# Contiguous block transposes of the probabilities, V's rows loaded to match them, and a new order of steps in a fused attention and expert kernel

## The chip, the cores and the metric

The kernel runs on 1 core of one Trainium2 chip. The metric is the device time of one launch in microseconds; the kernel before takes 739.89 us, the median of 3 runs (739.19 to 741.18). Each engine of the core runs its own instructions in order and waits on semaphores for the others: TensorE (PE in the profile, with its weight loads as PEld), VectorE (DVE), ScalarE (ACT), GpSimd (POOL), and SyncE (SP), which here issues nearly all DMA transfers.

## The reference, cut to what is computed

```python
B, H, S, D = 8, 8, 576, 64                     # pool = 8, so 72 keys for each head
k_p = k.reshape(B, H, 72, 8, D).mean(axis=3)
v_p = v.reshape(B, H, 72, 8, D).mean(axis=3)
scores = (q @ k_p.transpose(0, 1, 3, 2)) / sqrt(D)
attn = exp(scores - max(scores)); attn = attn / (sum(attn) + 1e-9)
x = (attn @ v_p).transpose(0, 2, 1, 3).reshape(4608, 512)
a = x @ w1; b = x @ w2                          # 512 -> 1024 each
out = ((a * b) @ w3) @ w_out                    # 1024 -> 1024 -> 512
```

All inputs and the output are fp32.

## The kernel before

**Numbers.** Every operand of a product is split into a rounded high part and the rest, and three products (high by high, high by low, low by high) stand for one in fp32. So nearly every result of PE is followed by a cast on ACT (the high part, `*_hi`, `*_post`) and a subtraction on DVE or POOL (the low part, `*_lo`).

**Stages.** The 4608 tokens are 12 chunks of 384. From the start to about 83 us W = w3 @ w_out is made (`w_turn`, `w_mm`; the conversions are `high`, `low`, `conv_b`, `ro_hi`, `ro_lo`, where `low` runs on DVE at L199 or on ACT at L196). Chunks 0 to 3 then run plain: `ab` (a and b, twelve matmuls of 128 x 384 each per block of 128 hidden columns), `a_post`, `b_post` (L807, a times b), `g_hi` (L812), `g_lo` (L817), `out_t` (L835). Chunks 4 to 11 run in pairs from about 320 us: seven block products stand for eight (`prod`, L976), on sums of the weights' blocks that were mixed before (`mix_sum`, `mix`, `plain_out`) and written to DRAM, one tensor `ws` for each block j of hidden columns. `load_u` (L958) brings them back into a ring of 5 buffers of 512 KB (and one of 256 KB); a load waits until the products have left its buffer. The last stage writes the rest of the output.

**Attention of a chunk** runs ahead of its expert stage, between the other steps: scores (`s_mm`), softmax (`soft1`, `soft_e`, `soft_s`, `soft2`; on the tiles in `SOFT_ACT` part of it runs on ACT), then the probabilities are turned so that keys lie on partitions. A pair of heads has 144 keys: the middle 128 are `main`, and the 16 outer ones of all four pairs are gathered into R (`soft3`, `soft4`). For chunks 0 and 1 PE turns them. For the others `te_turn` does it on DVE, as 32 x 32 blocks: one instruction for `main` at L674, which reads the keys interleaved (`(e k)`, k = 4), and two for R at L677. `te_in` (L696) then spreads the blocks over the partitions by DMA, `te_post` splits them, and `av_mm` (L739) multiplies by V's pooled means: `vbd`, block-diagonal for a pair of heads, with a high part (`prep_v2`, L494, ACT) and a low part (`prep_v3`, L499, DVE or POOL), and `VR` for the outer keys (`prep_vr2`). `load_v` (L471) loads half of a batch's V by one 512 KB transfer; `pool_tree` sums groups of 8 rows.

**What sets the order.** Each step is put into `plan` by `at(kind, k, fn, args)`, and a table, `SEQUENCE`, a permutation of the plan's indices, gives the order in which all steps are written; each engine, SP's transfers included, runs its instructions in that order. A second table, `OTHER`, moves single steps to another engine (`on()`: from DVE to POOL; `low` and `out_post`: from DVE to ACT). Output rows leave through a ring of 3 buffers: `out_post` (L866 on ACT, L868 on DVE) copies and at once issues the store (L869).

Of the kernel before, what the change touches and what calls it, by code (L numbers as in the profile page):

```python
# [19 lines left out]
def kernel(  # L20
# [48 lines left out]
        "mix": {(0, 0), (1, 1), (3, 0), (4, 0), (4, 1), (5, 0), (5, 1), (7, 0), (7, 1)},  # L69
        "mix_sum": {(0, 0), (1, 0), (1, 1), (2, 0), (3, 0), (3, 1), (4, 0), (4, 1), (5, 0), (5, 1), (6, 1), (7,  # L70
            0)},
        "out_post": {(0, 0), (0, 1), (0, 2), (1, 1), (1, 2), (2, 1), (2, 2), (3, 1), (3, 2), (4, 0), (4, 2), (5,
            0), (5, 1), (6, 0), (6, 2), (7, 0), (7, 2), (8, 0), (8, 2), (9, 1), (10, 0), (10, 1)},
        "prep_k": {(0, 1), (1, 0), (1, 1), (2, 0), (2, 2), (3, 0), (3, 1), (3, 2), (4, 1), (4, 3), (5, 0), (5,
            1), (5, 2), (5, 3), (6, 0), (6, 2), (6, 3), (7, 0)},
        "prep_v": {(0, 0), (0, 1), (1, 0), (2, 0), (2, 1), (3, 0), (5, 0), (5, 1), (6, 1), (7, 1)},
        "prep_v3": {(0, 0), (1, 0), (1, 1), (2, 1), (3, 0), (4, 0), (4, 1), (7, 0), (7, 1)},
        "prep_vr": {(0,), (1,), (2,), (3,), (5,), (6,), (7,)},
        "prep_vr2": {(0,), (1,), (2,), (3,), (7,)},
        "r3_low": {(0,), (1,), (2,), (4,), (13,), (15,)},  # L80
        "ro_lo": {(4,), (5,), (7,)},
        "ro_low": {(0,), (1,), (2,), (3,), (5,), (7,)},
        "soft4": {(0, 0), (0, 1), (1, 2), (2, 0), (2, 2), (3, 1), (5, 1), (5, 2), (6, 0), (6, 1), (7, 0), (7,
            2), (7, 3), (8, 0), (8, 1), (8, 2), (9, 2), (10, 0), (10, 1), (10, 3), (11, 2)},
        "t_lo": {(0, 0), (0, 1), (1, 0), (1, 1), (2, 1), (3, 0), (3, 1), (4, 0), (5, 1)},
        "t_low": {(0, 0), (0, 1), (1, 1), (3, 1), (5, 1)},
        "vr_sub": {(1,)},
# [29 lines left out]
    msk = small.tile([P, 16], F32, name="msk")[:, :4]  # L117
# [351 lines left out]
    def load_v(b, hf):  # L469
        t = stage["v", b, hf] = st_tile([P, 2, POOL, D])  # L470
        nc.sync.dma_start(out=t.rearrange("k a e d -> k a (e d)"), in_=pair_rows(v, b)[KR:KR + P, 2 * hf:2 * hf + 2])  # L471
# [126 lines left out]
    def soft2(n, t):  # L598
        b, off, nt = tok_tiles(n)[t]
        E, sm = Et[n, t], Mt.pop((n, t))[1]  # L600
        nc.vector.tensor_scalar(
            out=sm[:nt], in0=sm[:nt], scalar1=1e-9, scalar2=float(POOL), op0=ALU.add, op1=ALU.mult)
# [60 lines left out]
    def te_turn(n, t):  # L663
# [6 lines left out]
        if x == 0:  # L670
# [185 lines left out]
    def out_post(m, t):  # L856
# [12 lines left out]
        nc.sync.dma_start(out=out[r0:r0 + P], in_=ob)  # L869
# [354 lines left out]
    for m in range(NP):  # L1224
# [29 lines left out]
    for M in range(NP // 2, NCH // 2):  # L1254
# [78 lines left out]
    for b in range(1, B):  # L1333
# [189 lines left out]
```

## Time and profile before

| what | value |
|---|---|
| median of 3 runs | 739.89 us |
| the profiled execution | 740.11 us |
| its span | 738.3 us |
| TensorE busy | 720.7 us (98%) |
| VectorE busy | 523.8 us (71%) |
| ScalarE busy | 362.1 us (49%) |
| GpSimd busy | 189.1 us (26%) |
| DMA queue 1, share of 16 engines | 63.0% |

A time is the whole execution; the span, from the first to the last recorded instruction, is 1.8 us shorter. The profile names groups of instructions by line, engine, operation and tiles (out<-in), and gives for an idle stretch of an engine the instruction of another engine or the transfer that ended it. PEclk is the granted TensorE clock as a share of full speed.

### The profile page before, as it was taken

The page shows a single profiled execution, that of the slowest core. Times are in us where ns is not written, and L with a number is a line of the kernel's source. Part 1 is how long each engine was busy: PE and PEld are TensorE (multiplying, and loading weights), DVE is VectorE, ACT ScalarE, POOL GpSimd, SP SyncE. Part 2 cuts the span into 40 slices and gives each one's busy share as a digit, 9 for nine tenths or more (in the row PEclk, how much of TensorE's full clock was granted, in tenths as well). Part 3 has the DMA queues.
Part 4 walks back from the last instruction along what each step waited for, and adds up shares of the span by engine and source line. Part 5 has one row for each costly group of instructions (what it writes and reads, how often), then busy time and mean ns, then how long its engine had stood idle before and what let it go on. Part 6 is the DMA issues. An engine that isn't in the chain of part 4 may idle for free.

```text
span 738.3 us, 12016 instructions
## 1 busy us (share of the span) xinstructions
PE 720.7 (98%) x3992; PEld 665.9 (90%) x3992; DVE 523.8 (71%) x1042; ACT 362.1 (49%) x1140; POOL 189.1 (26%) x241
## 2 busy tenths in 40 slices
PE   7999999999999999998999999999999999999997
PEld 6788989899989999998999899899898999899996
DVE  3988898869767968887568877488887576643342
ACT  6888786534334544663355553355554254421221
POOL 2343865434506506203313011220030100000000
PEclk9999999999999999999999999999999999999999
DMA  9999590174457556798785739966358563166511
GB/s 320 348 285 288 154 255 30 59 205 118 108 141 249 155 152 194 198 293 224 221 263 151 186 106 277 252 204 175 86 194 276 139 208 115 34 228 233 173 35 69
DMA packets 138733, 136.59 MB, mean 185 GB/s; under 512 B 76080, under 2 KB 104240, under 8 KB 138672
## 3 DMA queue, kind: packets, MB, share of 16 engines
q1 hardware_dynamic: 138528, 135.69, 63.0%
q8 instruction: 32, 0.52, 0.3%
q14 instruction: 29, 0.24, 0.1%
q10 hardware_dynamic: 144, 0.13, 0.1%
HBM read 99.35 MB, written 24.12 MB: 167 GB/s over the span
## 4 chain that ended last, share of the span: by engine, by line
PE 78%; DVE 9%; DMA 4%; POOL 4%; ACT 3%; issue 2%; SPq 0%; DVEq 0%; POOLq 0%; ACTq 0%
PE a L976 17%; PE o L835 14%; PE att L976 8%; PE o L851 8%; PE a L787 6%; PE b L787 6%; PE b L976 5%; PE att L543 4%; PE att L739 4%; PE o L1068 3%; DMA ring<-ws 2%; DMA PTx<-T 1%; DVE mx L559 1%; POOL VR L530 1%; DMA raw<-in_moe_w_out_dram 1%
## 5 line engine op out<-in xcount | busy, mean ns | idle before, releaser
L976 PE MATMUL a<-X,ring 128*128 128x384 f32 x768 | 157.0, 340 | 1.4 <-DVE g L1009 0.7
L976 PEld LDWEIGHTS a<-X,ring 128*128 128x128 f32 x768 | 134.7, 189 | 7.0 <-DVE g L1009 1.7
L835 PE MATMUL o<-Wc,gh 128*128 128x512 f32 (+1 forms) x384 | 118.6, 390 | 0.0
L581 ACT ACTIVATE E<-att,mx 128x72 f32<-128x72 f32 (+1 forms) x264 | 80.7, 324 | 32.8 <-DVE mx L559 21.2
L482 POOL TENSOR_TENSOR st<-st 72x512 f32<-72x512 f32 (+2 forms) x32 | 42.7, 1335 | 162.0 <-DMA st<-in_v_dram 101.3
L835 PEld LDWEIGHTS o<-Wc,gh 128*128 128x128 f32 x384 | 70.2, 188 | 11.7 <-DVE ob L868 0.2
L976 PE MATMUL att<-X,ring 128*128 128x384 f32 x384 | 78.6, 341 | 2.0 <-DMA ring<-ws 2.0
L835 PE MATMUL o<-Wc,gl 128*128 128x512 f32 (+1 forms) x192 | 74.6, 389 | 1.2 <-DVE gl L817 1.1
L787 PE MATMUL b<-xT,hl 128*128 128x384 f32 x384 | 73.2, 340 | 0.1
L787 PE MATMUL a<-xT,hl 128*128 128x384 f32 x384 | 72.4, 337 | 0.0
L976 PEld LDWEIGHTS att<-X,ring 128*128 128x128 f32 x384 | 68.0, 190 | 3.5 <-DVE R L630 2.4
L787 PEld LDWEIGHTS a<-xT,hl 128*128 128x128 f32 x384 | 66.7, 188 | 0.5
L787 PEld LDWEIGHTS b<-xT,hl 128*128 128x128 f32 x384 | 66.2, 188 | 0.7 <-DVE a L807 0.4
L851 PE MATMUL o<-Wc,gh 128*128 128x512 f32 x192 | 61.6, 393 | 0.0
L817 DVE TENSOR_TENSOR gl<-a,gh 128x384 fp32r<-128x384 f32 x64 | 41.1, 646 | 22.7 <-ACT gh L812 18.2
L581 ACT ACTIVATION_READ_ACCUMULATOR E<-att,mx 128x1 f32 (+1 forms) x264 | 55.2, 209 | 0.0
L812 ACT CAST gh<-a 128x384 fp32r<-128x384 f32 x64 | 33.0, 517 | 43.8 <-DVE a L1004 14.9
L543 PE MATMUL att<-kbd,qT 128*128 128x144 f32 (+1 forms) x320 | 49.3, 286 | 0.6 <-DVE qT L390 0.6
L543 PEld LDWEIGHTS att<-kbd,qT 128*128 128x128 f32 (+1 forms) x320 | 45.3, 179 | 2.9 <-DVE qT L390 0.9
L835 PEld LDWEIGHTS o<-Wc,gl 128*128 128x128 f32 x192 | 36.0, 188 | 10.2 <-DVE gl L817 2.6
L559 DVE TENSOR_REDUCE mx<-att 128x4 f32<-128x288 f32 (+1 forms) x80 | 34.9, 448 | 14.4 <-PE att L543 14.3
L982 ACT COPY a<-a 128x384 f32<-128x384 f32 x32 | 15.3, 479 | 51.5 <-PE a L976 51.3
(164 smaller groups left out, 1348.7 us busy)
## 6 DMA issues: line engine op xcount, KB each, us to landing
ring<-ws SPq DMA_DIRECT2D x81, 512.0 KB
raw<-in_moe_w_dram SPq DMA_DIRECT2D x32, 512.0 KB
ws<-hl SPq DMA_DIRECT2D x24, 512.0 KB
out_dram<-ob SPq DMA_DIRECT2D x35, 256.0 KB
st<-in_v_dram SPq DMA_DIRECT2D x16, 512.0 KB
PTx<-T SPq DMA_DIRECT2D x28, 288.0 KB
ring<-ws SPq DMA_DIRECT2D x29, 256.0 KB
st<-in_k_dram SPq DMA_DIRECT2D x24, 288.0 KB
```

What stands on the lines that cost most here:

```text
L482: eng.tensor_tensor(out=t[:, :, 0:4], in0=t[:, :, 0:4], in1=t[:, :, 4:8], op=ALU.add)
L543: nc.tensor.matmul(out=ps[:nt, 2 * KP * j:2 * KP * (j + 1)], lhsT=qT[n][:, pr, off:off + nt], rhs=kbd[b % 2][:, pr], start=True, stop=True,)
L559: nc.vector.tensor_reduce(out=mx[:nt, hs], in_=sv, axis=AX.X, op=ALU.min)
L581: nc.scalar.activation(out=E[:nt, h], in_=sv[:, i], func=AF.Exp, scale=-1.0, bias=mx[:nt, h:h + 1], accum_out=sm[:nt, h:h + 1])
L739: nc.tensor.matmul(out=Tp[n, pr, "x"][:, off:off + cnt], lhsT=parts[x][0], rhs=parts[x][1], start=x == 0, stop=x == 3)
L787: nc.tensor.matmul(out=o, lhsT=w12[j, w][:, kt, sw], rhs=x[sx][:, kt], start=(i == 0), stop=(i == 3 * NK - 1))
L812: nc.scalar.copy(out=gh, in_=g)
L817: eng.tensor_tensor(out=gl, in0=g, in1=f(gh), op=ALU.subtract)
L835: nc.tensor.matmul(out=o, lhsT=(gh, gl)[sg][:, c], rhs=W[j][sw][:, d], start=(j == 0 and i == 0), stop=(j == NJ - 1 and i == 2))
L851: nc.tensor.matmul(out=oacc[m][t], lhsT=(gh, gl)[sg][:, t * P:(t + 1) * P], rhs=W[j][sw], start=(j == first and i == 0), stop=(j == last a ...
L976: nc.tensor.matmul(out=o, lhsT=w[:, kt, sw], rhs=x[sx][:, kt], start=first and n == 0, stop=n == 5, skip_group_check=True)
L1068: nc.tensor.matmul(out=wacc[h][it], lhsT=w3t[s][sa][:, it * P:(it + 1) * P], rhs=wo[j][sb], start=(j == 0 and i == 0), stop=(j == NJ - 1 a ...
```

## The change

- `te_turn`: for batches b >= 2 `main` is read as it lies, so a block of 32 neighbouring keys is turned as a block (30 of the 33 tiles). The two instructions for R become one of twice the size, on all 33 tiles.
- `load_v`: for b >= 2 V's rows are loaded in the order that this gives the keys, as two transfers of 256 KB in place of one of 512 KB (12 more transfers).
- `prep_v2`, `prep_v3`: with that order the two heads of a pair are no longer in the two halves of the partitions, so for b >= 2 both run over all 128 partitions and multiply by a mask per row (`halves()`, made once by a DVE reduction). `prep_v3` is then on DVE always.
- `soft2`: for n >= 2 and tiles in `SOFT_ACT` (27 tiles) the scaling of the sums moves from DVE to ACT.
- `out_post`: the store of an output tile becomes a step of its own, `out_st`, with its own place in the order (33 stores; those of the last chunk follow their copy as before).
- `OTHER` is dealt anew, and `SEQUENCE` is a new permutation.

Over the kernel PE keeps 3834 instructions; DVE goes from 1044 to 991, ACT from 879 to 910, POOL from 246 to 236, SP from 569 to 581.

```diff
-        "prep_v3": {(0, 0), (1, 0), (1, 1), (2, 1), (3, 0), (4, 0), (4, 1), (7, 0), (7, 1)},
+        "prep_v3": {(0, 0), (0, 1)},
...
-        "ro_low": {(0,), (1,), (2,), (3,), (5,), (7,)},
+        "ro_low": {(1,), (6,)},
...
     def load_v(b, hf):
         t = stage["v", b, hf] = st_tile([P, 2, POOL, D])
-        nc.sync.dma_start(out=t.rearrange("k a e d -> k a (e d)"), in_=pair_rows(v, b)[KR:KR + P, 2 * hf:2 * hf + 2])
+        src = pair_rows(v, b)[KR:KR + P, 2 * hf:2 * hf + 2]
+        if b < 2:
+            nc.sync.dma_start(out=t.rearrange("k a e d -> k a (e d)"), in_=src)
+            return
+        for a in range(2):
+            nc.sync.dma_start(
+                out=t[:, a].rearrange("k e d -> k (e d)"), in_=src[:, a].rearrange("(k p) c -> p k c", k=4))
...
+    def halves():
+        if "halves" not in stage:
+            m = stage["halves"] = masks[:, 4:6]
+            nc.vector.tensor_reduce(
+                out=m, in_=ident.rearrange("p (c j e) -> p j c e", j=2, e=2), axis=AX.XY, op=ALU.add)
+        return stage["halves"]
+
     def prep_v2(b, par):
+        if b >= 2:
+            nc.scalar.mul(
+                out=vbd[b % 2][0][:, :, D * par:D * par + D], in_=vm[b], mul=halves()[:, par:par + 1])
+            return
...
     def prep_v3(b, par):
+        if b >= 2:
+            hi, lo = (vbd[b % 2][s][:, :, D * par:D * par + D] for s in range(2))
+            nc.vector.scalar_tensor_tensor(
+                out=lo, in0=vm[b], scalar=halves()[:, par:par + 1], in1=f(hi), op0=ALU.mult, op1=ALU.subtract)
+            return
...
-        nc.vector.tensor_scalar(
-            out=sm[:nt], in0=sm[:nt], scalar1=1e-9, scalar2=float(POOL), op0=ALU.add, op1=ALU.mult)
+        if n < NT or (n, t) not in SOFT_ACT:
+            nc.vector.tensor_scalar(
+                out=sm[:nt], in0=sm[:nt], scalar1=1e-9, scalar2=float(POOL), op0=ALU.add, op1=ALU.mult)
+        else:
+            nc.scalar.activation(
+                out=sm[:nt], in_=sm[:nt], func=AF.Copy, scale=float(POOL), bias=1e-9 * POOL)
...
         nc.vector.transpose(
-            out=T[:, :, :NPR].rearrange("p k a e -> p a k e"), in_=main.rearrange("p a (e k) -> p a k e", k=4))
-        for s in range(2):
-            nc.vector.transpose(
-                out=T[:, 2 * s:2 * s + 2, NPR:],
-                in_=R[:nt, s].rearrange("p (r e) -> p r e", r=2).unsqueeze(1).broadcast_to([nt, 2, 2, 32]))
+            out=T[:, :, :NPR].rearrange("p k a e -> p a k e"),
+            in_=main.rearrange("p a (e k) -> p a k e", k=4) if b < 2 else main)
+        nc.vector.transpose(
+            out=T[:, :, NPR:],
+            in_=R[:nt].rearrange("p s (r e) -> p s r e", r=2).unsqueeze(2).broadcast_to([nt, 2, 2, 2, 32]))
...
-        nc.sync.dma_start(out=out[r0:r0 + P], in_=ob)
+        stage["ob", m, t] = ob
+        if m == NCH - 1:
+            out_st(m, t)
+
+    def out_st(m, t):
+        r0 = m * CH + t * P
+        nc.sync.dma_start(out=out[r0:r0 + P], in_=stage.pop(("ob", m, t)))
...
     SEQUENCE = (
...
```

**Where the order changes: SP at the start of the pair stage.** A ring load of block j names `ws_93` (j = 0), `ws_94` (j = 1), `ws_95` (j = 2); `st` are K's and V's rows. `ring_3967` of before and `ring_3937` of after are read by the first att product of j = 1, `ring_3942` of before by a product of j = 2. Before:

```order
L958 DMA ring_3871<-ws_93 128x1024
L901 DMA ws_99<-hl_3864 128x4x256
L958 DMA ring_3919<-ws_93 128x1024
L407 DMA st_3921<-in_k_dram 72x2x512
L958 DMA ring_3942<-ws_95 128x1024
L407 DMA st_3953<-in_k_dram 72x2x512
L958 DMA ring_3965<-ws_93 128x512
L958 DMA ring_3967<-ws_94 128x1024
```

and after:

```order
L991 DMA ring_3871<-ws_93 128x1024
L408 DMA st_3911<-in_k_dram 72x2x512
L991 DMA ring_3913<-ws_93 128x1024
L991 DMA ring_3937<-ws_94 128x1024
L902 DMA out_0_dram<-ob_3908 128x512
L991 DMA ring_3966<-ws_93 128x512
L484 DMA st_3972<-in_v_dram 16x1x512 x4
L991 DMA ring_3985<-ws_94 128x1024
```

The first ring load of `ws_94` has moved from the fifth ring load of the group to the third, ahead of the 256 KB load; the load of `ws_95` has left the group, and an output store and four small loads of V's outer rows have come into it.

**ACT before the first product with batch 2's V** (chunk 3; `vm` is the pooled V, `gh` the high part of a times b, `xT0` the high part of that product's result). Before:

```order
L797 COPY a_2465<-a_2450 128x384
L893 CAST hl_2467<-mix_2156 128x4x128
L706 CAST PTh_2406<-PTx_2407 128x768
L812 CAST gh_2520<-a_2465 128x384
L494 CAST vbd0_0_103<-vm_1937 64x4x64
L765 CAST xT0_2533<-att_2528 128x384
```

and after:

```order
L839 CAST gh_2217<-a_2160 128x384
L507 ACTIVATE vbd0_0_103<-vm_1996,msk_109 128x4x64 x2
L824 COPY a_2243<-a_2230 128x384
L599 ACTIVATE E_2189<-E_2189 128x288
L926 CAST hl_2266<-mix_1974 128x4x128
```

The second high part of `vbd` stood right before the cast of the product's first result; now both stand together, and that cast (`xT0_2543`) follows 25 rows later.

**DVE at that same place.** After, the low parts of `vbd` are on DVE, the second right before the subtraction that makes the low part of the product's result:

```order
L734 TENSOR_TENSOR PTx_2392<-PTx_2392,PTh_2391 128x2x384
L895 COPY ob_2497<-o1_2051 128x512
L834 TENSOR_TENSOR a_2492<-b_2499,a_2492 128x384
L517 SCALAR_TENSOR_TENSOR vbd0_1_104<-vm_1996,msk_109,vbd0_0_103 128x4x64
L799 TENSOR_TENSOR xT1_2544<-att_2538,xT0_2543 128x384
```

Before, one of the two was on POOL, behind POOL's `mix` and `VR` work.

**DVE early in the start stage** (`wt` and `Wc` hold raw and converted weights). Before:

```order
L203 SCALAR_TENSOR_TENSOR Wc<-Wc 128x512
L199 TENSOR_SCALAR Wc<-raw 128x512
L203 SCALAR_TENSOR_TENSOR wt<-wt 128x512 x2
L203 SCALAR_TENSOR_TENSOR Wc<-Wc 128x512
L243 TENSOR_TENSOR hl<-wt,hl 128x512
```

and after:

```order
L204 SCALAR_TENSOR_TENSOR Wc<-Wc 128x512
L204 SCALAR_TENSOR_TENSOR wt<-wt 128x512
L200 TENSOR_SCALAR wt<-raw 128x512
L204 SCALAR_TENSOR_TENSOR wt<-wt 128x512
L204 SCALAR_TENSOR_TENSOR Wc<-Wc 128x512
L244 TENSOR_TENSOR hl<-wt,hl 128x512
```

Two of the `wt` low parts that ACT made (L196) are now made by DVE itself (L200), in the same stretch.

## Rows read from the trace of the kernel before

**Rows 1.** Windows: stretch, us, busy of each engine (x instructions), PEclk, DMA share, GB/s.
```profile
83.00:140.00 57.00, 54.28 (x331) 50.25 (x330) 53.45 (x99) 37.89 (x138) 38.35 (x43) 1.00 0.42 117
140.00:330.00 190.00, 188.44 (x1055) 177.40 (x1055) 147.89 (x300) 90.45 (x314) 66.10 (x90) 1.00 0.61 174
330.00:350.00 20.00, 18.01 (x94) 17.28 (x93) 15.69 (x36) 8.42 (x37) 6.09 (x8) 0.91 0.88 239
350.00:570.00 220.00, 217.84 (x1199) 201.87 (x1198) 165.00 (x345) 107.14 (x369) 40.82 (x53) 1.00 0.69 198
sum 738.30, PE 720.72 PEld 665.90 DVE 523.85 ACT 362.14 POOL 189.07; mean PE 90.09 PEld 83.24 DVE 65.48 ACT 45.27 POOL 23.63
```

**Rows 2.** Waits of PE: line waited for, us in total, times, longest us.
```profile
PE att L976 <- DMA ring<-ws: 2.0, 1, 2.0
PE att L739 <- POOL vbd L499: 1.2, 1, 1.2
PE att L255 <- DVE Wc L203: 1.1, 1, 1.1
PE att L739 <- ACT vbd L494: 0.8, 1, 0.8
PE b L976 <- DMA ring<-ws: 0.7, 1, 0.7
```

**Rows 3.** Timeline of PE around 341 us: start, us, instructions [idle before].
```profile
341.67 2.26 PE L976 MATMUL att<-X,ring 128*128 128x384 f32 x6 [1.99 <-DMA ring<-ws]
343.73 1.81 PE L976 MATMUL a<-X,ring 128*128 128x384 f32 x6
345.37 1.20 PE L976 MATMUL att<-X,ring 128*128 128x384 f32 x6
346.41 1.20 PE L976 MATMUL a<-X,ring 128*128 128x384 f32 x6
```

**Rows 4.** Timeline of SP before that wait: start, us, ring loads issued.
```profile
329.12 0.32 SPq L958 DMA_DIRECT2D ring<-ws  x1
...
331.15 2.89 SPq L958 DMA_DIRECT2D ring<-ws  x2
```

**Rows 5.** The chain that ended last: start us, us, its two ring loads.
```profile
333.72 7.82 DMA ring<-ws
...
462.76 9.02 DMA ring<-ws
```

**Rows 6.** Groups of DVE by form: xcount | busy us, mean ns | idle before.
```profile
L674 DVE STREAM_TRANSPOSE T<-E 128x512 f32<-128x512 f32 x21 | 22.9, 1092 | 0.1
L390 DVE STREAM_TRANSPOSE qT<-qs 128x384 f32<-128x384 f32 x28 | 14.8, 557 | 0.7 <-DMA qs<-in_q_dram 0.7
L677 DVE STREAM_TRANSPOSE T<-R 128x128 f32<-128x128 f32 x42 | 9.8, 274 | 0.0
```

**Rows 7.** Line 601: ns min/median/max, first and last start, forms.
```profile
L601 DVE TENSOR_SCALAR sm<-sm x40: 151/165/1504, 53.7 to 602.0; 128x8 f32<-128x8 f32 x24, 96x8 f32<-96x8 f32 x16
```

**Rows 8.** Line 499, the low part of vbd, by engine, in the same columns.
```profile
L499 POOL TENSOR_TENSOR vbd<-vm,vbd x9: 713/737/1053, 69.1 to 559.8; 64x256 fp32r<-64x256 f32 x9
L499 DVE TENSOR_TENSOR vbd<-vm,vbd x7: 370/422/810, 66.6 to 515.2; 64x256 fp32r<-64x256 f32 x7
```

**Rows 9.** Line 471, issue of V's loads on SP, in the same columns.
```profile
L471 SPq DMA_DIRECT2D st<-in_v_dram x16: 384/416/1361, 36.2 to 533.8; - x16
```

**Rows 10.** Timeline of ACT at 207 us.
```profile
207.60 0.51 ACT L812 CAST gh<-a 128x384 fp32r<-128x384 f32 x1 [1.55 <-DVE a L807]
208.02 0.40 ACT L494 CAST vbd<-vm 64x256 fp32r<-64x256 f32 x1
```

**Rows 11.** Waits of SP, with those for output copies.
```profile
SPq L869 <- ACT ob L866: 38.5, 11, 12.6
```

**Rows 12.** Timeline of DVE in the start stage.
```profile
20.14 0.69 DVE L203 SCALAR_TENSOR_TENSOR wt<-wt 128x512 int32<-128x512 int32 x1 [0.65 <-ACT wt L196]
21.25 0.69 DVE L203 SCALAR_TENSOR_TENSOR wt<-wt 128x512 int32<-128x512 int32 x1 [0.42 <-ACT wt L196]
```

More of the change, by code (lines that the diff above doesn't have):

```diff
@@ L68 @@
     OTHER = {
[L69 to L75, printed above, removed]
@@ L76 @@
-        "prep_v": {(0, 0), (0, 1), (1, 0), (2, 0), (2, 1), (3, 0), (5, 0), (5, 1), (6, 1), (7, 1)},
-        "prep_v3": {(0, 0), (1, 0), (1, 1), (2, 1), (3, 0), (4, 0), (4, 1), (7, 0), (7, 1)},
[L78 to L81, printed above, removed]
-        "ro_low": {(0,), (1,), (2,), (3,), (5,), (7,)},
-        "soft4": {(0, 0), (0, 1), (1, 2), (2, 0), (2, 2), (3, 1), (5, 1), (5, 2), (6, 0), (6, 1), (7, 0), (7,
-            2), (7, 3), (8, 0), (8, 1), (8, 2), (9, 2), (10, 0), (10, 1), (10, 3), (11, 2)},
@@ L85 @@
-        "t_lo": {(0, 0), (0, 1), (1, 0), (1, 1), (2, 1), (3, 0), (3, 1), (4, 0), (5, 1)},
-        "t_low": {(0, 0), (0, 1), (1, 1), (3, 1), (5, 1)},
-        "vr_sub": {(1,)},
+        "mix": {(0, 1), (1, 1), (2, 0), (3, 0), (3, 1), (4, 0), (4, 1), (5, 0), (5, 1), (6, 0), (7, 0), (7, 1)},
+        "mix_sum": {(0, 0), (1, 1), (2, 0), (3, 0), (3, 1), (4, 0), (4, 1), (5, 1), (6, 0), (7, 0), (7, 1)},
+        "out_post": {(0, 0), (2, 0), (2, 1), (2, 2), (3, 0), (3, 1), (3, 2), (4, 0), (4, 1), (4, 2), (6, 1), (7,
+            2), (8, 1), (8, 2), (9, 0), (10, 0), (10, 1)},
@@ new lines @@
+        "prep_k": {(0, 0), (1, 1), (1, 2), (2, 1), (2, 2), (3, 0), (3, 1), (4, 1), (4, 2), (4, 3), (5, 0), (5,
+            1), (5, 3), (6, 0), (6, 1), (6, 3), (7, 0), (7, 1)},
+        "prep_v": {(0, 0), (0, 1), (1, 0), (2, 1), (3, 0), (4, 0), (5, 0), (5, 1), (7, 1)},
+        "prep_v3": {(0, 0), (0, 1)},
+        "prep_vr": {(0,), (3,), (5,), (6,), (7,)},
+        "prep_vr2": {(0,), (1,), (3,), (5,)},
+        "r3_low": {(0,), (1,), (2,), (3,), (5,), (8,), (9,), (10,), (11,), (12,), (13,), (15,)},
@@ new lines @@
+        "ro_lo": {(1,), (5,), (6,)},
+        "ro_low": {(1,), (6,)},
+        "soft4": {(0, 1), (1, 1), (1, 2), (2, 0), (3, 0), (5, 1), (6, 0), (6, 1), (7, 0), (7, 1), (7, 3), (8,
+            0), (8, 1), (8, 2), (9, 2), (10, 3), (11, 1)},
+        "t_lo": {(0, 0), (0, 1), (1, 0), (1, 1), (2, 1), (3, 0), (3, 1), (4, 1), (5, 1), (6, 0), (6, 1), (7, 0),
+            (7, 1)},
+        "t_low": {(1, 0), (1, 1), (2, 1), (5, 0), (5, 1), (6, 0), (7, 0), (7, 1)},
+        "vr_sub": {(0,), (1,), (5,)},
@@ L116 @@
     VR = [cp.tile([P, NPR, P], F32R, name=f"VR{i}") for i in range(2)]
-    msk = small.tile([P, 16], F32, name="msk")[:, :4]
+    masks = small.tile([P, 16], F32, name="msk")
+    msk = masks[:, :4]
     neg = cp.tile([P, P], F32R, name="neg")
@@ L1236 @@
             at("P", m0 + 3 * NJ + 3 + 2 * (m == NP - 1), out_post, m, t)
+            at("P", m0 + 3 * NJ + 3 + 2 * (m == NP - 1), out_st, m, t)
     M1 = M0 + 3 * NJ * NP
@@ L1275 @@
             at("P", k + 1, out_post, 2 * M, t)
+            at("P", k + 1, out_st, 2 * M, t)
         for j in range(NJ):
@@ L1282 @@
                 at("P", k + 5 + NJ, out_post, 2 * M + 1, t)
+                at("P", k + 5 + NJ, out_st, 2 * M + 1, t)
     free = {n: [M2 - 1] * (SLOTS if n == 2 else 1) for n in (1, 2)}
```

290 rows, old and new, of the table SEQUENCE are left out of this document.

## The prediction, made before the changed kernel ran

> **What bounds the kernel now.** I read the windows first. Over the span PE is busy 720.72 of 738.30 us, so every other engine is cover and only PE's idle time, 17.58 us, can be saved, besides stretches where its clock is low [rows 1]. DVE is dense in places: 53.45 of 57 us from 83 to 140, where PE loses 2.72; but from 140 to 330 it is busy 147.89 of 190, and PE loses only 1.56 [rows 1]. From 83 to 570 PE's idle is 2.72 + 1.56 + 1.99 + 2.16 = 8.43 us [rows 1]. Then I read PE's waits: five single ones (2.0, 1.2, 1.1, 0.8, 0.7) are most of what can be named outside the first loads and the end [rows 2]. The wait of 2.0 is for a ring load at the start of the pair stage, and the granted clock of that stretch is 0.91 [rows 1, 2].
>
> **The change, part by part.** PE's instructions are the same in number and form, so no work of PE goes; the sum is of waits.
>
> *Ring load at 341.67.* PE idles 1.99 us, and the next two groups of six take 2.26 and 1.81 us busy where the same six take 1.20 right after [rows 3]: another (2.26 + 1.81) − 2 × 1.20 = 1.67. The granted clock of 0.91 over these 20 us [rows 1] is 0.09 × 20 / 0.5 = 3.6 us at the lower level, 1.2 GHz, before the six are back at 1.20. Together 3.66. The load that ended it was issued last of a group of five on SP, at 333.72, and took 7.82 to land [rows 5]; in the new order it is the third of the group. The spot of the third was issued at 329.12 [rows 4], so it would land at 336.9, before 341.67 − 1.99 = 339.68. The next in line is then `ring_3985` in the last spot: it lands near 341.5 and is read two groups of six later, 339.68 + 2 × 1.04 = 341.8 (six start 1.04 apart, 346.41 − 345.37 [rows 3]). I take the whole 3.66; the margin of 0.2 is the weakest of the sum. Bounds 0 to 3.7.
>
> *Second ring wait, 0.7* [rows 2]. That load took 9.02 us [rows 5]. Counting matmuls in the order, between the product that frees a buffer and the one that reads the reload, at 1.04 / 6 = 0.173 us each [rows 3], it had some 30, 5.1 us, the fewest before the last stretch; the one above had 34, 6.0 us. After, the fewest there are 38, 6.6 us. Gain 0.7, bounds 0 and 0.7.
>
> *V's low part on POOL, 1.2.* At 131 us PE waits for a `vbd` subtraction that stood on POOL behind `mix` and `VR` work [rows 2]; POOL's takes 737 ns and DVE's 422 [rows 8]. It is on DVE now and stands well before the product. Gain 1.2, bounds 0 and 1.2.
>
> *V's high part on ACT, 0.8.* At 208.02 the second cast of `vbd` ran after the `gh` cast, which had waited 1.55 us for DVE [rows 10]; PE waited for it [rows 2]. After, both masked casts stand together, 25 rows of ACT ahead of the first cast of the product's result. Gain 0.8. In their place the second low part stands on DVE right before the subtraction of that product: if DVE is late there, PE waits for it, as it did on POOL for 1.2 [rows 2]. Bounds −1.2 to 0.8.
>
> *Start stage, 1.1.* PE's wait for `Wc` [rows 2] follows two waits of DVE for ACT's low parts, 0.65 and 0.42 [rows 12]. Two of these are on DVE now, so DVE waits less and works a little more. I take 0.8, nearer to the upper end since PE's wait is as long as the two waits of DVE together; bounds 0 to 1.1.
>
> *DVE's lighter work: nothing by itself.* The transpose of `main` takes 1092 ns; a contiguous one of 384 columns takes 557, and with the slope to the 128-column one, (557 − 274) / 256 = 1.1 ns a column, 512 would take 557 + 141 = 698 [rows 6]. So 30 × 0.39 = 11.8 us of DVE go, from bounds of 0 (the pattern costs nothing) to 30 × 0.53 = 16 (as cheap as 384 columns). The two R transposes of 274 become one of about 274 + 141 = 415: 33 × 0.13 = 4.4 us. The 27 scalings moved to ACT take 27 × 0.165 = 4.5 us off [rows 7]. All this lies after 138 us, where DVE is busy three quarters of the time and PE loses under 1% [rows 1]; where DVE is dense, before 140, it hardly begins. The dealing of `OTHER` spends part of it again. If that cover were gone, the whole 20 us could not return more than the idle that is there. I count 0, bounds 0 to 1.
>
> *V's masks.* ACT's masked high part covers 128 partitions with 256 columns as the old one covered 64; I cost it at the 0.40 of the old [rows 10]. ACT is busy under half of the time [rows 1]. DVE's masked low part I cost at 422 ns [rows 8]; 12 of them, 6 of which were on POOL, add 6 × 0.42 = 2.5 us to DVE, less than it loses. One reduction for the masks, once. Hidden: 0. The row of 810 ns [rows 8] shows a DVE low part that took twice the median, so the bound is 12 × 0.39 = 4.7 us of DVE, of which the second of each of 6 batches stands close before the product: 6 × 0.39 = 2.3 us on PE at the worst.
> That row bears on a page that speaks against the change: the Trainium skill, "SBUF — State Buffer", section "Who interferes with whom", has a DVE instruction with two SBUF inputs contend with a GpSimd instruction that reads SBUF, and the low part is such an instruction, now 12 times on DVE. By the median the sum stays at 734.7; by the rule at its worst it would be 737.0, inside the forecast's range; I give it 0.1 of the forecast's chance. The trace's 370 to 810 ns is consistent with it but names no cause [rows 8].
>
> *Twelve more transfers for V.* 12 × 0.416 = 5.0 us of SP's issue [rows 9], between 138 and 534 us, each at most 0.4 ahead of a ring load. V is loaded far ahead of its use; a ring load queued directly behind pays 0.4. Count 0, bounds −1 to 0.
>
> *Output stores as steps.* SP waited 38.5 us in 11 waits for ACT's output copies, the longest 12.6 [rows 11], with loads queued behind. Neither ring load that PE waited for was behind such a store [rows 4], so 0; a store ahead of `ring_3966` is new, so bounds −1 to 0.
>
> *New waits.* The named middle waits take 2.0 + 1.2 + 0.8 + 0.7 = 4.7 of 8.43; the other 3.7 is small change of the order that I cannot name, and a new permutation of everything brings its own. I add 2 us, between 0 and 7 (as much again as the named gains); 2, since 3.7 of the same kind was there and DVE has more room now.
>
> Sum: −3.66 − 0.7 − 1.2 − 0.8 − 0.8 = −7.2, + 2 = −5.2. From the profiled 740.11: 734.9. The median stands 0.2 below that execution, so **734.7 us**.
>
> **The rivals.**
> *Nothing arrives.* Each wait removed is followed by another of about its size: the product that followed the late one was itself only just fed, as `ring_3985`'s margin of 0.2 suggests. For it: 98% busy leaves little slack anywhere, and the low-clock stretch comes back with any wait of that length at that place [rows 1, 3]. Against it: the waits have five different causes, and three of them go by a change of queue. Gains 7, new waits 7: 739.9.
>
> *Slower: the ring runs late at the start of the pair stage.* There DMA is at 0.88 [rows 1]. In the new order `ring_3871` and `ring_3913` have 38 matmuls each, 6.6 us, between the release of the buffer and the use. If a load lands as the slow one did, 9.02 us [rows 5], each waits 2.4 us, with 1.67 of lower clock behind it [rows 3]: 2 × 4.1 = 8.2. The gains without the first ring wait are 3.5, new small waits 2: with both late 8.2 − 3.5 + 2 = +6.7, 746.6; with one, 4.1 − 3.5 + 2 = +2.6, 742.5. It decides when loads there take more than about 8 us. For it: 7.82 was measured in this stretch. Against it: `ring_3871` of before had a like distance and PE did not wait for it. I take one late, 742.5.
>
> *All gains, no new waits:* 739.9 − 7.2 = 732.7, an end of the forecast's own range.
>
> **How the numbers follow.** What a measurement of this kernel can tell from no change is about 0.3%, 2.2 us: 737.7 to 742.1. The forecast with its bounds (732 to 737.5) has 0.70, the first rival 0.17, the second 0.13. The range goes from 731.5 (all gains, and a microsecond from DVE's room) to 740.5 (the first rival); beyond it are the ring running late and a little more gain than named. Faster 0.70, the same 0.17, slower 0.13.
>
> **What would show it.** Right: no PE wait for `ring` near 340 and PEclk of 1.00 there; no PE wait for `vbd`; the transpose of `main` near 0.70 us and that of R near 0.42; PE busy near 719 (the low clock gone) and idle near 14. Wrong: new waits of PE for `ring`, for DVE's `vbd` or for `g` that add up to over 4 us, or a second stretch of lower clock. If DVE's saving shows as PE time, PE's waits for DVE rows between 140 and 570 will have gone below what is named here.

## The result, and the profile after

The changed kernel takes 748.5 us (median of 4 runs, 745.56 to 751.12) beside 740.06 for the kernel before in the same runs: 1.0112 of it, 95% interval 1.0072 to 1.0152. Forecast was 734.7, range 731.5 to 740.5. The change made the kernel slower by 8.4 us where 5.2 us less were expected. The profiled execution below is the one of 751.12 us, the longest of the four, so its waits are read for their place and cause, and what a wait is worth is taken from the experiments.

Windows of the changed kernel, in the columns of [rows 1]; the first two stretches and the sum are added:

```profile
0.00:26.00 26.00, 20.86 (x109) 18.00 (x110) 12.58 (x22) 18.35 (x33) 5.33 (x14) 0.93 0.95 333
26.00:83.00 57.00, 54.84 (x291) 45.10 (x290) 44.26 (x80) 45.66 (x117) 28.06 (x31) 1.00 0.93 278
83.00:140.00 57.00, 52.56 (x309) 48.82 (x307) 51.96 (x91) 40.17 (x141) 32.83 (x33) 0.97 0.43 120
140.00:330.00 190.00, 187.05 (x1040) 176.61 (x1041) 138.52 (x274) 87.95 (x303) 72.29 (x96) 0.99 0.58 160
330.00:350.00 20.00, 16.25 (x87) 15.81 (x86) 11.65 (x26) 10.11 (x47) 0.32 (x1) 0.83 0.87 253
350.00:570.00 220.00, 219.43 (x1210) 203.84 (x1209) 160.87 (x332) 108.80 (x392) 45.00 (x55) 1.00 0.71 194
sum 749.30, PE 726.23 PEld 671.52 DVE 507.56 ACT 367.01 POOL 184.47; mean PE 90.78 PEld 83.94 DVE 63.45 ACT 45.88 POOL 23.06
```

DVE is busy 16.3 us less than before (507.56 beside 523.85), as the edits promise, and PE still loses. From 350 to 570 PE is better fed than before (219.43 of 220, 217.84 in [rows 1]). The loss stands in four stretches. In 83 to 140, 140 to 330 and 330 to 350 the granted clock is lower too; in the last of them PE idles 3.75 us and the clock is 0.83. The fourth is 26 to 83, in the start stage, where PE was nearly never idle before:

```profile
26.00:83.00 57.00, 56.85 (x310) 47.99 (x309) 48.80 (x88) 46.34 (x119) 30.20 (x32) 1.00 1.03 288
```

By stretch PE's idle time has grown by 0.2 (0 to 26), 2.0, 1.7, 1.4 and 1.8 us and fallen by 1.6 (350 to 570), together 5.5; PE's busy time is 5.5 longer for the same instructions (726.23 beside 720.72), which goes with the lower clock (0.989 over the span beside 0.997). The longest waits of PE (columns as in [rows 2]):

```profile
PE a L1009 <- DMA ring<-ws: 4.1, 2, 3.8
PE a L814 <- DVE hl L307: 3.5, 1, 3.5
PE att L254 <- DVE Wc L204: 2.6, 2, 2.2
PE att L766 <- ACT PTh L733: 2.2, 1, 2.2
```

The start stage's waits for `Wc` are no better than in [rows 2]. Of the four waits of the middle that the prediction removed, the ring load of [rows 3] and `vbd` on POOL and on ACT are gone, and the second ring wait is down to 0.3. Three others, larger, have come.

**The ring, at 338 us.** PE (start, us, instructions [idle before]):

```profile
338.31 2.26 PE L1009 MATMUL a<-X,ring 128*128 128x384 f32 x6 [3.75 <-DMA ring<-ws]
340.37 2.12 PE L566 MATMUL att<-kbd,qT 128*128 128x144 f32 x8
342.12 1.87 PE L1009 MATMUL att<-X,ring 128*128 128x384 f32 x6
343.83 1.20 PE L1009 MATMUL a<-X,ring 128*128 128x384 f32 x6
```

and SP before it (start, us, transfers issued):

```profile
322.98 0.37 SPq L934 DMA_DIRECT2D ws<-hl  x1
329.24 0.33 SPq L408 DMA_DIRECT2D st<-in_k_dram  x1
329.66 0.32 SPq L991 DMA_DIRECT2D ring<-ws  x1
330.04 1.96 SPq L376 DMA_DIRECT2D qs<-in_q_dram  x4
332.09 0.94 SPq L991 DMA_DIRECT2D ring<-ws  x2
```

SP issues nothing from 323.35 to 329.24. It stands at a load of K's rows, whose staging buffer is the one that the write `ws<-hl` just ahead of it reads: the mixed weights `hl` and the rows `st` take turns in one pool of 4 buffers, and the step order fixes whose turn it is. Behind the load stand three ring loads, issued at 329.66 and 332.09; the one that PE waits for is of the first block, `ws_92`. (In the code `ws_92` is block j = 0, so each j in the section on the change is one too low for its tensor.) The chain that ended last shows the write and the ring load that PE waited for (start, us):

```profile
322.98 6.25 DMA ws<-hl
332.09 6.09 DMA ring<-ws
```

After the wait, six matmuls take 2.26 and 1.87 us and then 1.20 again: the lower clock.

**DVE, at 121 us.** PE waits for the low part of a block of weights (`hl`, L307), which stands on DVE right behind one softmax step:

```profile
115.89 4.11 DVE L631 TENSOR_TENSOR E<-E,sm 96x576 f32<-96x576 f32 x1
119.92 1.20 DVE L307 TENSOR_TENSOR hl<-wb,hl 128x512 fp32r<-128x512 f32 x1
```

That instruction takes 0.757 us as a rule (median of 40) and here 4.11. POOL runs in the same time, with gaps under 0.1 us:

```profile
116.18 0.73 POOL L537 TENSOR_TENSOR st<-st 32x256 fp32r<-32x256 f32 x1
116.89 2.49 POOL L307 TENSOR_TENSOR hl<-wb,hl 128x512 fp32r<-128x512 f32 x2
119.45 2.26 POOL L914 TENSOR_TENSOR mix<-hl 128x256 f32<-128x256 f32 x2
```

**A late output store, at 177 us.** PE's wait of 2.2 us for `PTh` is the end of a chain through four engines. Rows of DVE, SP, POOL and ACT, in order of time (start, us, instruction [idle before]):

```profile
154.76 0.68 DVE L895 COPY ob<-o 128x512 f32<-128x512 f32 x1
```
```profile
161.32 1.77 SPq L902 DMA_DIRECT2D out_dram<-ob  x2
```
```profile
167.29 0.76 DVE L914 TENSOR_TENSOR mix<-hl 128x256 f32<-128x256 f32 x2 [4.20 <-DMA out_dram<-ob]
```
```profile
170.65 0.74 POOL L920 TENSOR_TENSOR mix<-mix 128x256 f32<-128x256 f32 x1 [17.93 <-DVE mix L914]
...
175.52 0.45 POOL L491 TENSOR_TENSOR km<-st 72x128 f32<-72x128 f32 x1
```
```profile
176.00 0.62 ACT L926 CAST hl<-mix 128x512 fp32r<-128x512 f32 x1 [3.62 <-POOL km L491]
176.52 0.83 ACT L733 CAST PTh<-PTx 128x768 fp32r<-128x768 f32 x1
```

An output tile is copied at 154.76, but its store, now a step of its own, is the second of the two issued from 161.32, behind transfers of other work and the store of a tile copied at 160.30. The late store shifts the turns in the pool of 3 buffers that output tiles and mix tiles share. In `e4_store`, where stores go out with their copies, the tile of 160 us takes the buffer of the tile of 154 us, and the next mix tile takes one that is already free; here, by the buffer addresses of the two programs, the tile of 160.30 takes that free buffer, and the mix tile gets it next. So DVE waits 4.2 us, not for the late store but for the one of the tile of 160.30, which had only just been issued. The sum that POOL waits for stands behind that mix on DVE, POOL then sums K late, the K rows hold the buffer of the next `hl`, and ACT's cast of the probabilities stands behind that `hl`.

**The start stage, 26 to 83 us.** Four new waits of 1.12, 0.47, 0.19 and 0.31 us stand between 35 and 43 us; the longest:

```profile
35.79 0.50 PE L1101 MATMUL o<-hl 128*128 128x512 f32 x1 [1.12 <-DVE hl L262]
```

This loss is no chance of one execution. In the nine profiled runs with the new order PE is busy 54.6 to 55.1 us of these 57, in the five with the old one 56.3 to 56.9. It comes with the order or the dealing and not with the edits of code (`e2_order` below has 54.8, `e1_edits` 56.6). No experiment moves a single step there, so which step it is stays open.

### The profile page after: what moved, and what is told of

It reads as the page before. It is cut to its first block, busy times and chain, and to the rows that moved or that the text cites. A ratio compares the mean times of both kernels' runs of the same rounds, so it can differ in the third digit from the quotient of the medians.

```text
span 749.3 us, 11935 instructions
## 1 busy us (share of the span) xinstructions
PE 726.2 (97%) x3992; PEld 671.5 (90%) x3992; DVE 507.6 (68%) x989; ACT 367.0 (49%) x1171; POOL 184.5 (25%) x231
## 4 chain that ended last, share of the span: by engine, by line
PE 79%; DVE 8%; DMA 6%; ACT 4%; issue 1%; SPq 1%; POOL 1%; DVEq 0%; POOLq 0%; ACTq 0%
PE a L1009 17%; PE o L862 14%; PE att L1009 9%; PE o L878 8%; PE a L814 6%; PE b L814 5%; PE att L566 5%; PE b L1009 4%; PE att L766 4%; PE o L1101 3%; DMA ring<-ws 3%; DVE wb L204 1%; DMA ws<-hl 1%; DMA out_dram<-ob 1%; DMA raw<-in_moe_w_out_dram 1%
## 5 line engine op out<-in xcount | busy, mean ns | idle before, releaser
L814 PE MATMUL a<-xT,hl 128*128 128x384 f32 x384 | 74.8, 345 | 3.5 <-DVE hl L307 3.5
L814 PEld LDWEIGHTS a<-xT,hl 128*128 128x128 f32 x384 | 68.8, 194 | 4.4 <-DVE hl L307 3.8
L489 POOL TENSOR_TENSOR st<-st 72x512 f32<-72x512 f32 (+2 forms) x29 | 40.5, 1396 | 73.9 <-DMA st<-in_v_dram 41.6
L844 DVE TENSOR_TENSOR gl<-a,gh 128x384 fp32r<-128x384 f32 x64 | 38.0, 597 | 25.2 <-ACT gh L839 16.7
L657 POOL TENSOR_TENSOR R<-E,R 128x64 fp32r<-128x64 f32 (+1 forms) x20 | 7.6, 388 | 176.3 <-ACT R L652 101.9
```

The costliest lines, as they stand in the source:

```text
L489: eng.tensor_tensor(out=t[:, :, 0:4], in0=t[:, :, 0:4], in1=t[:, :, 4:8], op=ALU.add)
L814: nc.tensor.matmul(out=o, lhsT=w12[j, w][:, kt, sw], rhs=x[sx][:, kt], start=(i == 0), stop=(i == 3 * NK - 1))
L844: eng.tensor_tensor(out=gl, in0=g, in1=f(gh), op=ALU.subtract)
```

## The experiments

Medians are set beside the ratio to the kernel before, run in turn on the same chip. The runs fall into sets on different chips, so between sets the ratios compare, and the medians only roughly.

**The edits alone, the order alone.** `e1_edits` is the kernel before with the new bodies of `te_turn`, `load_v`, `prep_v2`, `prep_v3` and `soft2`; `e2_order` is the changed kernel with the old bodies, so "order" here takes in the new dealing and the stores as steps.

```diff
 e1_edits (from the kernel before)
-            out=T[:, :, :NPR].rearrange("p k a e -> p a k e"), in_=main.rearrange("p a (e k) -> p a k e", k=4))
+            out=T[:, :, :NPR].rearrange("p k a e -> p a k e"),
+            in_=main.rearrange("p a (e k) -> p a k e", k=4) if b < 2 else main)
...
 e2_order (from the kernel after): the same lines the other way
```

> The kernel before, in its own order and with its own dealing of steps to engines, with the edits of code alone: contiguous transposes, V loaded by rows to match, masks, the scaling of the sums on ACT; stores stay with their copies. Theory (the order costs, the edits are worth about nothing on PE): 738.5 to 741.5, within 0.2% of 740.06, with DVE busy some 16 us less than 523.8. Rival (the edits cost: the masked low part or the new DVE-ACT-DVE round in the softmax holds PE): 743 to 749, with PE waits for vbd or for E that the kernel before does not have.

> The changed kernel's order and dealing, with the old code of the transposes, V's loads, prep_v2, prep_v3 and soft2. Theory (the order costs): 746 to 752, with the PE waits of the changed kernel at 121, 177 and 338 us still there, as DVE is no freer. Rival (the edits cost): 738 to 742.

`e1_edits`: 737.79 us, 0.9964 (0.9936 to 0.9992). `e2_order`: 755.29 us, 1.0198 (1.0141 to 1.0255). Both lie outside their theory's band, below 738.5 and above 752, but on its side: the order costs, and the edits do not, they are a small gain in the old order. They are also no cover in the new one: without them it is another 6.8 us slower by the medians, though the intervals of the two ratios just overlap.

**The load of K's rows.** `e3_kload` moves one entry of `SEQUENCE`:

```diff
 SP's order in e3_kload (from the kernel after)
 DMA ws_99<-hl
-DMA st<-in_k_dram
 DMA ring<-ws_93
 DMA qs<-in_q_dram x4
 DMA ring<-ws_92
 DMA ring<-ws_92 (256 KB)
+DMA st<-in_k_dram
```

> The changed kernel with one step moved: the load of K's rows that SP holds for 6.25 us (its staging buffer is the one that the write to ws just ahead of it reads) now stands behind the ring loads of j = 0 instead of ahead of them. Theory (that load held the ring loads behind it on SP): the PE wait of 3.75 us at 338.3 goes, and with it 1.06 + 0.97 + 0.67 us of lower clock: 748.5 - 6.4 = 742.1, PEclk of 330 to 350 back to 1.00. Rival (DMA at 0.87 there brings the load late anyhow): under 2 us gained, 746.5 to 748.5, the wait still over 2 us.

741.36 us, 1.0015 (0.9993 to 1.0038): 7.1 us gained, the theory (by the ratios 0.0097 of 740 us, 7.2, give or take 3.4). SP now issues the ring load right after the write, and PE is not held:

```profile
319.58 0.37 SPq L934 DMA_DIRECT2D ws<-hl  x1
320.05 0.45 SPq L991 DMA_DIRECT2D ring<-ws  x1
```
```profile
330.00:350.00 20.00, 19.96 (x119) 19.03 (x118) 16.57 (x36) 13.34 (x65) 3.29 (x5) 1.00 0.92 276
```

The second fence is its window from 330 to 350: PE busy 19.96 of 20 at full clock, with DMA at 0.92, busier than in the changed kernel. The transfers were not slow; one waited in front of them.

**The stores.** `e4_store` issues each store with its copy; `e5_both` adds the move of `e3_kload`.

```diff
-        stage["ob", m, t] = ob
-        if m == NCH - 1:
-            out_st(m, t)
+        nc.sync.dma_start(out=out[r0:r0 + P], in_=ob)
```

> The changed kernel with each output store issued by its copy's step, as before the change, and no out_st steps; all else in its place. Theory (a store that comes late holds the buffer which the next mix tile takes): DVE's wait of 4.2 us at 162 to 167 for an output store goes, POOL's 35.9 us of waits for stores go, and PE's wait of 2.2 + 0.55 us for te_post at 177 with its lower clock (the next groups take 1 us longer): 748.5 - 3.5 = 745. Rival (the K sums on POOL are late for another reason): the wait at 177 stays, 747.5 to 749.

> The changed kernel with both moves at once: the load of K's rows behind the ring loads, and the stores issued by their copies. Theory (two separate waits, and each measured alone): 741.36 - (748.5 - 746.47) = 739.3, 738 to 741; what is left against the kernel before is PE's wait for the weights' low part at 121 us. Rival (the two gains are the same slack counted twice): 741 to 742.

`e4_store`: 746.47 us, 1.0074 (1.005 to 1.0098), 2.0 us less than the changed kernel, which its interval (from 1.0072) does not tell from nothing. In the trace the wait at 177 is gone, and DVE's for the store with it. That shows the chain, not what it costs. DVE's mix stands at once behind its other work:

```profile
162.93 0.75 DVE L911 TENSOR_TENSOR mix<-hl 128x256 f32<-128x256 f32 x2
```

POOL's waits for stores did not go, against the expectation (30.9 us, off the path). And a new wait has come. A later store, at 215.93, now holds SP for 7.3 us until its tile is copied; the loads of q stand behind it, and PE waits at 228 for q's transpose. SP, then the wait of PE:

```profile
207.20 1.36 SPq L938 DMA_DIRECT2D ws<-hl  x1
215.93 0.34 SPq L896 DMA_DIRECT2D out_dram<-ob  x1
216.77 7.63 SPq L376 DMA_DIRECT2D qs<-in_q_dram  x16
224.51 0.38 SPq L896 DMA_DIRECT2D out_dram<-ob  x1
```
```profile
PE att L566 <- DVE qT L391: 1.3, 1, 1.3
```

`e5_both`: 743.05 us, 1.0031 (1.0004 to 1.0058), not the 739.3 of the sum, and above the rival's 742 as well. With the ring mended, issuing all stores at once is worth nothing that these runs can tell; its interval overlaps that of `e3_kload`.

**DVE beside POOL.** Both start from `e5_both`. `e6_tlo` moves the awaited DVE step ahead of the stretched one; `e7_pool` takes POOL's work away at that time.

```diff
 DVE's order in e6_tlo
+L307 TENSOR_TENSOR hl<-wb,hl
 L625 TENSOR_SCALAR sm<-sm 96x8
 L630 RECIPROCAL sm<-sm 96x8
 L631 TENSOR_TENSOR E<-E,sm 96x576
-L307 TENSOR_TENSOR hl<-wb,hl
 OTHER in e7_pool
-        "mix_sum": {(0, 0), (1, 1), ...
-        "t_lo": {... (5, 1), (6, 0), (6, 1), (7, 0), (7, 1)},
+        "mix_sum": {(1, 1), ...
+        "t_lo": {... (5, 1), (7, 0), (7, 1)},
```

> The kernel e5_both with one step moved on DVE: the low part of a w1 block (t_lo of j = 5), for which PE waits 3.5 us at 121, stands ahead of a softmax step that took 4.11 us instead of 0.75, not behind it. Theory (PE waits only for what is queued behind the stretched instruction): the wait goes, with it 1.5 us of lower clock, 739.3 - 4.5 = 734.8. Rival (DVE is late anyhow, and what now stands behind, the softmax of chunk 1, is awaited as soon): 738.5 to 740, with a new wait of PE for E or for gl in 115 to 130.

> The kernel e5_both with three steps moved from POOL to DVE, where they stand later: two low parts of weights (t_lo of j = 6) and a sum for the mix, which POOL ran from 116.9 to 121.7, while one DVE instruction of 0.75 us took 4.11. Theory (DVE and POOL hold each other up when both read two tiles from SBUF): that DVE instruction is back under 1.6 us though its place is the same, PE's wait of 3.5 us shrinks under 1.0, 739.3 - 4 = 735.5. Rival (DVE was late for its own load): DVE, with 2 us more to do, makes PE wait as long or longer, 739 to 742.

`e6_tlo`: 743.58 us, 1.0032 (1.0002 to 1.0062): nothing gained on `e5_both` (both expectations started from 739.3, not from the 743.05 that `e5_both` took). The wait for the weights is gone, and PE waits 4.1 us a little later, for the softmax, which is the rival's sign. The hold has moved to whatever DVE instruction comes next, here a scaling of 96 x 8 that takes 0.17 us by the median:

```profile
117.07 3.83 DVE L625 TENSOR_SCALAR sm<-sm 96x8 f32<-96x8 f32 x1
```
```profile
PE att L679 <- ACT E L604: 4.1, 1, 4.1
```

`e7_pool`: 741.09 us, 0.9985 (0.9953 to 1.0018), and DVE, with more to do, is in time. The same instruction at the same place:

```profile
113.90 0.95 DVE L631 TENSOR_TENSOR E<-E,sm 96x576 f32<-96x576 f32 x1
114.78 1.22 DVE L307 TENSOR_TENSOR hl<-wb,hl 128x512 fp32r<-128x512 f32 x1
```

PE's wait for `hl` is 0.39 us instead of 3.5. POOL's neighbouring work held DVE up, and not DVE's own load. It is the trace that decides this; the time alone lies in the rival's band. The whole 4 us did not arrive: the gain is 2.0 us by the medians and 3.4 by the ratios, whose intervals overlap a little, and PE waits 1.48 us at 122 for q's transpose, which now stands behind the added DVE work. The two experiments together tell contention from a plain queue: moving the awaited step moved the hold, taking the neighbour away ended it.

**V's low part in the old order.** From `e1_edits`: `e8_vbd` puts the two low parts of batch 1 on DVE, as the change does; `e10_vpool` leaves them on POOL, one of them ahead of the mix and K sums it stood behind.

```diff
 e8_vbd
-        "prep_v3": {(0, 0), (1, 0), (1, 1), ...
+        "prep_v3": {(0, 0), ...
 POOL's order in e10_vpool
 L553 TENSOR_SCALAR VR<-vrh,msk x4
+L522 TENSOR_TENSOR vbd<-vm,vbd
 L914 TENSOR_TENSOR mix<-mix
...
 L491 TENSOR_TENSOR km<-st
-L522 TENSOR_TENSOR vbd<-vm,vbd
```

> The kernel e1_edits (the order of before with the edits of code), with the low parts of batch 1's V on DVE instead of POOL, the part of the new dealing that removes PE's wait of 1.2 us for POOL at 132. Theory: the wait goes, 737.8 - 1.2 = 736.6, and DVE, dense there, gives back under 0.5. Rival (DVE at 94% from 83 to 140 cannot take 0.8 us more): 737.8 or more, with new waits of PE for DVE before 140.

> The kernel e1_edits with the low part of batch 1's V left on POOL, but ahead of the mix and K steps it stood behind (it starts some 4.7 us earlier). Theory (PE's 1.2 us at 132 is a place in POOL's queue, and DVE was the wrong engine to move it to): the wait goes, 0.9964 - 0.0016 = 0.9948 of before. Rival (the softmax or the K sums behind it are awaited next): 0.996 to 0.999.

`e8_vbd`: 740.68 us, 0.9999 (0.997 to 1.0029). `e10_vpool`: 738.93 us, 0.9978 (0.9959 to 0.9997). Neither gains on `e1_edits`. In the first PE waits 1.6 us for the same tile, now on DVE, and 1.6 for `E` some 9 us earlier; in the second, 1.1 us for DVE four microseconds after the place of the old wait:

```profile
PE att L766 <- DVE vbd L522: 1.6, 1, 1.6
PE att L668 <- DVE E L631: 1.6, 1, 1.6
```
```profile
136.10 1.65 PE L814 MATMUL a<-xT,hl 128*128 128x384 f32 x8 [1.11 <-DVE hl L307]
```

So the wait of 1.2 us for POOL in [rows 2] was one face of a stretch that DVE bounds, and to remove it was worth nothing there that these runs can tell.

**The scaling of the sums.** `e9_dve` is `e1_edits` with the old `soft2`.

> The kernel e1_edits with the scaling of the softmax sums back on DVE (the transposes, V's row order and the masks stay). In e1_edits DVE waits 15.7 us in 14 waits for ACT's scaled sums, which no PE wait answers to. Theory (the edits' gain of 0.36% comes from the shorter transposes): the same as e1_edits, 0.995 to 0.998 of before. Rival 1 (the round through ACT costs what the transposes gain): 0.991 to 0.994. Rival 2 (the gain is DVE's 4.5 us of scalings): 0.998 to 1.001.

738.65 us, 0.998 (0.9967 to 0.9993). That lies on the line between the theory's band and the second rival's, and its interval overlaps that of `e1_edits`, so it doesn't tell which of the edits carries the small gain. It does show that the round through ACT neither costs nor gives much in the old order, though DVE waits 15.7 us for it in `e1_edits`.

**All places mended.** `e11_mix` is the changed kernel with the move of `e3_kload`, the dealing of `e7_pool` with those steps behind q's transposes, and only chunk 0's stores right behind their copies. `e12_old` is `e11_mix` with the old code bodies.

```diff
 e11_mix, moves in SEQUENCE
+load_k (5, 1) behind load_u (2, 0, 3)
+out_st (0, 0), (0, 1), (0, 2) each behind its out_post
+tr_q (2, 1) behind tr_q (2, 2), then t_lo (6, 0), t_lo (6, 1)
```

> The changed kernel with every place mended that the runs point to: the load of K's rows behind the ring loads; the stores of chunk 0 alone issued with their copies (in e4_store and e5_both later stores held SP ahead of the q loads and PE waited 1.4 us at 228); two weights' low parts and one mix sum from POOL to DVE, behind the transposes of q that PE waits for. Theory (the slowdown is these places and nothing else): 748.5 - 7 (K load) - 4.5 (contention at 121) - 2 (stores) = 735, 0.992 to 0.996 of before. Rival (the order loses in many small places): 0.998 or more.

> The kernel e11_mix (the mended order) with the old code of the transposes, V's loads, prep_v2, prep_v3 and soft2: what the edits of code are worth in an order that was laid out for them. Theory (the edits matter where an order is built on DVE's shorter work): e2_order stood 6.8 us above the changed kernel, so 735.6 + 5 to 8 = 741 to 744. Rival (DVE's time is cover in any good order): 735 to 738, as e1_edits gained 0.36% only.

`e11_mix`: 735.61 us, 0.9946 (0.9928 to 0.9964), the best of all kernels here: 12.9 us below the changed kernel and 0.5% below the kernel before. That is the theory's band, and the waits at 121, 177 and 338 are gone together (0.4 us is left of the first); which of the three moves gives how much in this mix was not run. Its largest group of PE's waits is 1.9 us, in the start stage, and from 140 to 330 PE has none at all. The start stage's loss remains: PE is busy 54.86 of 57 us from 26 to 83. The stretches behind it:

```profile
83.00:140.00 57.00, 53.75 (x322) 49.27 (x321) 52.68 (x100) 41.43 (x144) 27.32 (x28) 1.00 0.39 110
140.00:330.00 190.00, 190.00 (x1070) 179.67 (x1069) 138.68 (x279) 93.28 (x329) 72.00 (x96) 1.00 0.64 179
330.00:350.00 20.00, 19.97 (x112) 18.60 (x111) 16.82 (x36) 9.37 (x42) 8.30 (x10) 1.00 0.89 263
```

`e12_old`: 746.78 us, 1.0062 (1.0032 to 1.0092). The same order with the old code is 11.2 us slower by the medians and 8.6 by the ratios, where 5 to 8 were expected. In its trace the loss is spread: PE is busy 186.88 of 190 from 140 to 330, where `e11_mix` has 190.00, with waits of at most 1.0 us each for ACT and DVE, and 216.23 of 220 from 350 to 570, where `e11_mix` has 219.68. The edits are worth some 3 us in the order of before and 9 to 11 in this one; which of them carries it was not run.

## Why the prediction was wrong, point by point

**Where it failed.** The last term of the sum, "new waits, + 2", is the step that failed. It was not read from the new order; it was a size taken from the small waits of before, and 7 us were thought of as the sum of many, not as one event. The runs put 7.1 us on a single moved load and 2.0 to 3.4 on DVE beside POOL (`e5_both` to `e7_pool`). The stores' 2.0 is within the noise. The start stage idles 2.0 us more in the two profiles, and which step costs that is open. With the places at 121, 177 and 338 mended, the kernel is 12.9 us faster and below the kernel before, so new waits of this order, not the edits, made the change slower.

**The ring.** The prediction followed the group of five ring loads and stopped there. What stood ahead of the group on SP, and what that waited for, it did not follow: a load of K's rows whose buffer was still being read. The slower rival had the stage and the lower clock behind the wait right, though not the load (it named `ring_3871` and `ring_3913`, which are issued after the one that was late), and priced one late load at 4.1. PE's idle was 3.75, two groups of six lost 1.06 and 0.67, and the small ones between them about 1 more. But it gave another cause: it asked how long a load takes to land, and the measured landing of 6.09 us was below its point of decision of 8. A buffer shared by two kinds of tile decided it, not the transfer. The term of 3.66 was too large as well. `e1_edits` keeps the old order of SP, and there the same wait does not occur: PEclk of 330 to 350 is 1.00 and PE is busy 18.80. Nor does it in `e8_vbd`, `e9_dve` and `e10_vpool`, which keep that order too; they show at most 1.6 us for a ring load, on another product, and a clock of 1.00. The wait of [rows 3] was seen in one execution of the kernel before; it was a narrow race and no fixed cost.

**The second ring wait.** Nearly right: 0.7 us before, 0.3 after. No experiment separates its cause.

**V's low part on POOL.** The wait went, as forecast, in the changed kernel. As a gain of 1.2 it was wrong: `e8_vbd` and `e10_vpool` took POOL's wait away, and PE waited as long for DVE within some 9 us of the place. The row that spoke against it stood in the prediction, DVE busy 53.45 of 57 [rows 1]; a wait for POOL inside a stretch that DVE bounds is not free to collect.

**V's high part on ACT.** Right in kind: no wait of PE at that product in the changed kernel. But in the old order, with the edits alone, it is down to 0.2 us (`e1_edits`) and 0.4 (`e9_dve`) as well, so most of it did not need the new order.

**The start stage.** Not gained: PE's waits for `Wc` are 2.6 us after, where [rows 2] has one of 1.1 and the rest stood among the first loads, and from 26 to 83 PE idles 2.0 us more, 1.1 of it in one new wait for DVE (L262). So a term of −0.8 came out near +2. What the first 26 us cost changes from one execution to the next (PEclk is 0.87 to 1.00 in the nine profiled runs of the new order, 1.00 in that of the kernel before); the loss behind them does not, and no run tells which step brings it.

**DVE's lighter work.** The sizes were nearly right. The contiguous transpose was put at 698 ns and takes 754 and 690 by its two forms, R's merged one at 415 and takes 404:

```profile
L701 DVE STREAM_TRANSPOSE T<-E 128x512 f32<-128x512 f32 x21 | 15.8, 754 | 0.0
L704 DVE STREAM_TRANSPOSE T<-R 128x256 f32<-128x256 f32 x21 | 8.5, 404 | 0.0
```

What they are worth was put at 0, at most 1 us. In the old order it is 0.36%, some 2.7 us (interval 0.6 to 4.7), a little above the bound; in the mended order 9 to 11. "Nothing by itself" was read from the order of before. The new one needs the shorter work: without it PE waits in many small places. The worth of cover belongs to an order, not to an edit.

**V's masks.** Off the path, as said. ACT's masked part takes 510 ns, not 400; DVE's takes 476 by median and 993 at most, and PE has no wait for it in the changed kernel, 0.5 us in `e3_kload` and 0.4 in `e4_store`. The Trainium skill's rule, "SBUF — State Buffer", "Who interferes with whom", was weighed for these instructions only. The same rule holds at another place: the two-input softmax step at 115.89, beside POOL's reads, took 4.11 us, and 0.95 when POOL's work was taken away. The trace agrees with the page; the prediction put it to the instructions that the change added instead of to those which the new order put side by side (before, the same step took 1.12 us at most). In `e6_tlo` a scaling with one SBUF input was held as long, which the rule on two inputs does not cover by itself.

**V's transfers.** 24 issues of 602 ns (median) in place of 12 of 416: 14.4 − 5.0 = 9.4 us more of SP's time, not 5.0. None of PE's waits named above leads back to one.

**Stores as steps.** Put at 0, with a bound of 1 us. The reason given looked at what is queued behind a store on SP. It did not ask how a later store shifts the turns of the buffers that output tiles share with mix tiles. In the changed kernel DVE waits 4.2 us for a store, and PE idles 2.2 + 0.55 at 177; the kernel before has no such wait. What that costs in time stays within the noise. `e4_store` shows the other side: issued at once, a later store holds the loads of q.

## What to carry to other kernels

When a change is a new order, look for each transfer in the queue whose buffer was last used by something just ahead of it, and follow what stands behind it: one such load cost 7.1 us here, as much as all named gains were to bring together. Tiles of different kinds that share a pool tie engines together that the code never shows side by side; a store or a load moved for the sake of its queue also moves the moment at which its buffer comes free, and with it which tile takes which buffer. A wait removed in a stretch where another engine is dense can come back a few microseconds away, as it did here twice, and what an off-path saving is worth can only be said for a given order.

## What the runs showed of the hardware

At 116 to 120 us DVE finished no instruction for about 4 us while POOL ran sums and differences of two SBUF tiles one after another: a 0.757 us product took 4.11, and when the order was changed a scaling of 0.17 us in its place took 3.83. With four of POOL's instructions taken away, the first took 0.95. It is no rule that DVE stands still for as long as POOL does this. Three microseconds earlier in `e5_both` POOL ran two such instructions in 2.99 us, and DVE went on beside them, some of its instructions at twice their time (1.32 us beside 0.68). What makes the difference, no run here shows. A 32 x 32 block transpose of 512 columns that reads its blocks contiguously took 0.75 us where the interleaved read took 1.09 [rows 6].
